# Storing the dv and dk windows of a decode block's backward pass per kv-head

## The chip, the core and the metric

The kernel runs on one core of a Trainium2 chip. TensorE (PE) multiplies, VectorE (DVE) and ScalarE (ACT) work on tiles and empty PSUM, GpSimd (POOL) does some copies and starts transfers, SyncE (SP) only starts transfers. All transfers, whoever starts them, run on the core's 16 DMA engines. The time is device microseconds (us) of one execution; lower is better.

## The reference

One step of a transformer block is computed with its gradients, all in bfloat16, for a batch of B = 4 and one query position:

```python
xn = layernorm(x)                                  # x: [4, 1, 512]
q  = xn @ wq                                       # 32 heads of 128
k, v = last 1024 of the 4096 cached rows           # caches: [4, 8 kv-heads, 4096, 128]
o  = softmax(q k^T / sqrt(128)) v                  # 4 query heads share one kv-head
out = x + o @ wo + (gelu(xn @ w_gate) * (xn @ w_up)) @ w_down
```

The outputs are `out` and the gradients for x, k_cache, v_cache, wq, wo, w_gate, w_up and w_down. The gradients for the two caches (dk and dv) have the caches' full shape: 32 MiB each, of which 24 MiB belong to rows outside the window and are zero, and 8 MiB to the window of 1,024 rows per kv-head.

## The kernel before, in words

**Order of the work.** A feed-forward part (lines 249 to 373) comes first, then an attention part that runs over the four batch entries b (lines 380 to 638), then an end part (lines 640 to 735) that computes `out`, dx, dwo and dwq. A scheduler orders the instructions of PE, ACT, DVE and POOL from the order in the code and from priorities; only SP's queue is kept in the written order (line 78).

**Attention, per b.** `scores(0, b)` and `scores(1, b)` (line 471) transpose K and V with DVE and multiply; `softmax` (line 509) and `softmax_d` (line 536) make P and dS; `odq` (line 567) makes the output and dq; and `dvdk(0, b)` and `dvdk(1, b)` (line 550) make the window parts of dv and dk, 2 MiB for each call.

**dvdk.** For every pair of rows j, four PSUM banks (`kv_ps`, one for each c) receive 16 small matmuls, and `evac` (line 82) copies each bank to a staging tile with ACT or DVE, whichever its running count says is less loaded. A call uses two staging tiles (`stg`, 128 partitions of 8 KiB, four buffers in all, line 74): bank c holds kv-heads 2c and 2c+1, so the first tile has kv-heads 0 to 3 and the second 4 to 7, and every kv-head's part is complete only when the last j has been copied. In a tile, partition m holds, for each of its four kv-heads, eight window rows: 8 x 128 values, 2,048 bytes. Then `result` (line 112) stores the tile: it issues a transfer from POOL with `single_packet=True`. All other large results (dwd, dwu, dwg, dwo, dwq) go out through `result` and the same four staging buffers too.

**Loads.** `load_kv` (line 216) loads one b of K or V as two transfers of 1 MiB, four kv-heads each. The first K comes from SP's queue, all later loads from POOL's. Buffers: V has one (`va`), K two (`ka`, `kb`), so a load waits until `odq` has read the buffer for the last time. `refill` (line 462) is POOL work: eight small copies that lay out one b's query or output-gradient rows before `scores` uses them.

**Zeros.** The 48 MiB of zeros are written by 32 transfers of 1.5 MiB from SP's queue (`zeros`, line 236). They are spread over the kernel: each waits for the one two (later three) before it, and most also wait for a load's landing, or for a softmax or an `odq` to be done (lines 270, 381, 382, 621, 627, 629, 635, 637).

**Queues.** In the profile, q1 is SP's queue, q0 POOL's, q10 ACT's. A transfer from SBUF or to SBUF with 128 partitions is spread over the 16 DMA engines, eight partitions on each.

Of the kernel before, what the change touches and what calls it, by code (L numbers as in the profile page):

```python
# [18 lines left out]
def kernel(  # L19
# [27 lines left out]
    _, G, Sk, Dh = A_k_cache.shape  # L47
# [4 lines left out]
    K0 = Sk - W  # L52
# [7 lines left out]
    J = W // P  # L60
# [21 lines left out]
    def evac(out, in_, n):  # L82

        ca, cd = (190 + n) / 1.2, (130 + n) / 0.96
        eng = "act" if load["act"] + ca <= load["dve"] + cd else "dve"
        load[eng] += ca if eng == "act" else cd
        if eng == "act":
            return nc.scalar.copy(out=out, in_=in_)  # L88
        return nc.vector.tensor_copy(out=out, in_=in_)  # L89
# [11 lines left out]
    def stg_tile():  # L101
        return stage.tile([P, 4096], BF16, name="stg", tag="stg")

    def store(eng, out, in_, kind, apart, **kw):

        d = eng.dma_start(out=out, in_=in_, **kw)  # L106
        for k in apart:
            tc.declare_no_dep(d.ins, group=k, reason="stores write disjoint parts of the outputs")
        tc.add_to_no_dep_group(kind, d.ins)
        return d  # L110

    def result(out, in_):
        return store(nc.gpsimd, out, in_, "rest", ["zeros", "rest"], single_packet=True)

    def mm(out, lhsT, rhs, first=True, last=True, pos=None):
        kw = {} if pos is None else {"tile_position": pos}
        nc.tensor.matmul(out, lhsT=lhsT, rhs=rhs, start=first, stop=last, **kw)  # L117

    def bank(name, tag="w", shape=(P, 512), dt=FP32):
        pool = {"w": ps_w, "x": ps_x}.get(tag, ps_a)  # L120
        return pool.tile(list(shape), dt, name=name, tag=tag)
# [127 lines left out]
    with tc.tile_pool(name="ffn", bufs=1) as ffn:  # L249
# [76 lines left out]
        for h in range(2):  # L326
            stg = stg_tile()
# [9 lines left out]
        for wi, (wsb, dh, og) in enumerate(((wu_sb, dhu, out_7), (wg_sb, dhg, out_6))):  # L337
# [26 lines left out]
            for h in range(2):  # L364
                stg = stg_tile()
# [9 lines left out]
    with tc.tile_pool(name="mid", bufs=1, reuse_waits="tile") as mid:  # L375
# [4 lines left out]
        with tc.tile_pool(name="att", bufs=1, reuse_waits="tile") as att:  # L380
# [169 lines left out]
            def dvdk(k, b, sp, r_):  # L550

                og = (out_3, out_2)[k]
                stg = [stg_tile() for _ in range(2)]
                sv = [s_[:].rearrange("p (g j d) -> p j g d", g=4, j=J) for s_ in stg]
                for j in range(0, J, 2):
                    ps = [bank("kv_ps", "w", (P, 2, 2, Dh)) for _ in range(NQ)]
                    for u in range(2):
                        for c, q in enumerate(quad):
                            mm(ps[c][:, u].rearrange("p g d -> p (g d)"), sp[q, j + u].rearrange("p a m -> p (a m)"),
                               r_[q, b].rearrange("p g d -> p (g d)"), pos=(Q * c, 0))  # L560
                    for c in range(NQ):
                        evac(sv[c // 2][:, j:j + 2, (c % 2) * 2:(c % 2) * 2 + 2, :], ps[c][:], 512)
                for hf in range(2):
                    result(og[b, hf * 4:(hf + 1) * 4, K0:Sk, :].rearrange("g (m j) d -> m g (j d)", j=J),
                           stg[hf][:].rearrange("p (g e) -> p g e", g=4))

            def odq(k, b, pT):

# [44 lines left out]
            for b in range(B):  # L613
                S = scores(0, b)
                if b + 1 < B:
                    dP = scores(1, b)
                    refill(0, b + 1)
                    refill(1, b + 1)
                P_f, P_b, p_done = softmax(S)
                if b == B - 1:  # L620
                    zeros(3, p_done, 3)
                    turn_wq()
                    dP = scores(1, b)
                pT = turned(P_b, 0)
                o_done = odq(0, b, pT)
                if b + 1 < B:
                    zeros((2, 2, 4)[b], load_kv(b + 1, 1, att, "va", nc.gpsimd, single_packet=True))
                else:
                    zeros(2, o_done, 3)
                dvdk(0, b, spread(P_b, 0), rows[1])  # L630
                dS_b = softmax_d(P_f, dP)
                dST = turned(dS_b, 1)
                o_done = odq(1, b, dST)
                if b + 2 < B:
                    zeros(3, load_kv(b + 2, 0, (kap, att)[b % 2], ("ka", "kb")[b % 2], nc.gpsimd, single_packet=True))
                elif b == B - 1:
                    zeros(len(ztodo), o_done, 3)
                dvdk(1, b, spread(dS_b, 1), rows[0])

        with tc.tile_pool(name="end", bufs=1, reuse_waits="tile") as end:  # L640
# [14 lines left out]
            for n in range(KH):  # L655
                t, e, c = n // 8, n // 4 % 2, n % 4
# [59 lines left out]
            for t in range(4):  # L716
                stg = stg_tile()
# [9 lines left out]
            for c in range(C):  # L727
                stg = stg_tile()
# [37 lines left out]
```

## Time and profile before

Time: 285.05 us, median of 3 runs (284.68 to 286.16).

| of the profiled execution | |
|---|---|
| its own time | 284.82 us |
| span from first to last instruction | 283.0 us |
| PE, DVE, ACT, POOL busy | 66%, 58%, 44%, 21% of the span |
| DMA engines, packets' time: SP's queue q1 | 57.0% of 16 engines' span |
| DMA engines, packets' time: POOL's queue q0 | 40.8% of 16 engines' span |
| bytes moved | 112.21 MB (30.93 MB read from HBM, 81.01 MB written) |

How to read it: the page gives the busy share of every engine, then the span in 40 slices of 7.1 us with a digit for each engine (9 is 90% or more), then the DMA queues with their packets, bytes and the time that the packets took, then the chain of waits that ended last, and at last the costliest groups of instructions and the DMA issues with the median time from issue to landing. "out_dram<-stg" is a transfer from a staging tile to HBM, "out_dram<-ztile" one of zeros. A window can be asked for by itself, and then the shares are those of the window.

### The profile page before, as it was taken

Reading aid. Unit: us, or ns where it says so; the run is one execution under the profiler, and the core shown is the slowest. Engines: PE = TensorE matmul, PEld = TensorE weight load, DVE = VectorE, ACT = ScalarE, POOL = GpSimd, SP = SyncE. Lnnn points to the kernel's source line nnn. Section 1 sums busy time; section 2 is a strip of 40 time slices with the busy share of each in tenths; the row PEclk is TensorE's granted clock in tenths of the full one; section 3 lists DMA queues with packets and bytes.
Section 4 is the critical chain, followed back from the end, with each engine's and each line's share of the span. In section 5 each row is a group of like instructions: output and inputs, shape, how many; then the busy total and the mean of one; then the engine's idle time right before and its main releaser. Section 6 shows DMA issues by size and latency. Waiting matters only on the chain.

```text
span 283.0 us, 4400 instructions
## 1 busy us (share of the span) xinstructions
PE 187.6 (66%) x1731; PEld 76.8 (27%) x1733; DVE 165.0 (58%) x309; ACT 124.4 (44%) x245; POOL 60.3 (21%) x135
## 2 busy tenths in 40 slices
PE   0225989859544899759976663923357998944870
PEld 0102344233111543234331341311034232510210
DVE  4779674898798533635257254055496104396970
ACT  2032774740010469744725420802432767454870
POOL 8500000169075313120040060200020020201110
PEclk9999965556955555755555555555555555685555
DMA  6999989999999999999999999999999999999995
GB/s 217 430 446 435 432 317 420 424 430 396 392 428 406 383 357 425 328 365 411 421 419 414 408 427 405 396 422 421 429 382 423 413 410 403 399 415 396 391 397 223
DMA packets 16883, 112.21 MB, mean 396 GB/s; under 512 B 1368, under 2 KB 1632, under 8 KB 11104
## 3 DMA queue, kind: packets, MB, share of 16 engines
q1 hardware_dynamic: 6544, 66.46, 57.0%
q0 software_dynamic: 10176, 45.35, 40.8%
q8 instruction: 13, 0.21, 0.3%
q10 hardware_dynamic: 144, 0.13, 0.2%
q14 instruction: 6, 0.05, 0.0%
HBM read 30.93 MB, written 81.01 MB: 396 GB/s over the span
## 4 chain that ended last, share of the span: by engine, by line
DMA 30%; issue 14%; PE 13%; DVE 9%; ACT 3%; POOL 2%; POOLq 0%; ACTq 0%; DVEq 0%
DMA out_dram<-stg 30%; DVE scr L93 4%; PE kv_ps L117 4%; PE od_ps L117 3%; PE sc_ps L117 2%; PE dwq_ps L117 2%; ACT stg L88 2%; DVE stg L89 1%; POOL out_dram L106 1%; PE ok_ps L117 1%; PE es_ps L117 1%; DVE spr L492 1%; DVE dqs L593 1%; ACT E_f L524 1%; PE nm_ps L117 1%
## 5 line engine op out<-in xcount | busy, mean ns | idle before, releaser
L88 ACT CAST stg<-kv_ps 128x512 bf16<-128x512 f32 x118 | 63.6, 606 | 52.2 <-DMA out_dram<-stg 26.3
L106 POOL DMA_DIRECT2D out_dram<-stg x30 | 19.7, 659 | 150.0 <-ACT stg L88 94.7
L117 PE MATMUL sc_ps<-scr,bd 128*32 128x256 bf16 x256 | 24.2, 396 | 15.2 <-DVE scr L93 15.2
L117 PE MATMUL kv_ps<-qm,spr 32*128 32x256 bf16 x128 | 24.8, 385 | 13.0 <-ACT stg L88 12.5
L117 PE MATMUL kv_ps<-dm,spr 32*128 32x256 bf16 x128 | 28.9, 399 | 6.6 <-ACT stg L88 4.9
L93 DVE STREAM_TRANSPOSE scr<-va 128x1024 uint32<-128x1024 uint32 x16 | 18.9, 1219 | 12.9 <-DMA va<-in_A_v_cache_dram 12.8
L117 PEld LDWEIGHTS <-spr 32*128 32x128 bf16 x256 | 12.4, 102 | 46.4 <-issue 42.1
L89 DVE CAST stg<-kv_ps 128x512 bf16<-128x512 f32 x10 | 6.6, 683 | 17.0 <-PE kv_ps L117 11.0
L117 PEld LDWEIGHTS <-bd 128*32 128x32 bf16 x256 | 8.1, 107 | 29.1 <-issue 28.5
L88 ACT CAST stg<-dwg_ps 128x448 bf16<-128x448 f32 x26 | 12.7, 554 | 6.4 <-PE dwg_ps L117 5.5
L88 ACT CAST stg<-dwo_ps 128x512 bf16<-128x512 f32 x18 | 10.0, 588 | 11.4 <-PE dwo_ps L117 10.1
L117 PE MATMUL dwo_ps<-dy_b,oSP 32*128 32x512 bf16 x32 | 9.0, 508 | 7.5 <-ACT stg L88 6.2
L93 DVE STREAM_TRANSPOSE scr<-ka 128x1024 uint32<-128x1024 uint32 x8 | 9.6, 1228 | 5.2 <-DMA ka<-in_A_k_cache_dram 3.1
L222 POOL DMA_DIRECT2D va<-in_A_v_cache_dram x8 | 6.0, 757 | 27.3 <-PE od_ps L117 25.8
L93 DVE STREAM_TRANSPOSE scr<-kb 128x1024 uint32<-128x1024 uint32 x8 | 9.8, 1232 | 3.5 <-DMA kb<-in_A_k_cache_dram 2.9
L117 PE MATMUL do_ps<-scr,dyBD 128*128 128x512 bf16 x31 | 10.1, 459 | 2.4 <-DVE scr L93 2.1
L578 DVE SCALAR_TENSOR_TENSOR odt<-od_ps,oms,odt 128x128 f32<-128x128 f32 x4 | 1.4, 340 | 17.0 <-ACT odt L577 17.0
L117 PE MATMUL dwq_ps<-dqSP,xn_b 32*128 32x512 bf16 x32 | 10.7, 586 | 0.9 <-ACT stg L88 0.3
L89 DVE CAST stg<-dwq_ps 128x512 bf16<-128x512 f32 x15 | 9.9, 689 | 1.6 <-PE dwq_ps L117 1.4
L89 DVE CAST stg<-dwo_ps 128x512 bf16<-128x512 f32 x14 | 9.2, 680 | 2.7 <-PE dwo_ps L117 2.7
L117 PEld LDWEIGHTS <-pT 128*32 128x32 bf16 x256 | 9.2, 140 | 5.2 <-ACT pT L88 2.3
L88 ACT CAST stg<-dwq_ps 128x512 bf16<-128x512 f32 x17 | 9.7, 586 | 1.4 <-PE dwq_ps L117 0.7
(196 smaller groups left out, 321.3 us busy)
## 6 DMA issues: line engine op xcount, KB each, us to landing
out_dram<-ztile SPq DMA_DIRECT2D x32, 1536.0 KB, 12.1
out_dram<-stg POOLq DMA_DIRECT2D x24, 1024.0 KB, 13.7
va<-in_A_v_cache_dram POOLq DMA_DIRECT2D x8, 1024.0 KB, 17.6
out_dram<-stg POOLq DMA_DIRECT2D x6, 896.0 KB, 10.2
wq_sb<-in_A_wq_dram SPq DMA_DIRECT2D x1, 4096.0 KB, 25.6
wo_sb<-in_A_wo_dram SPq DMA_DIRECT2D x1, 4096.0 KB, 36.7
kb<-in_A_k_cache_dram POOLq DMA_DIRECT2D x4, 1024.0 KB, 19.4
ka<-in_A_k_cache_dram SPq DMA_DIRECT2D x2, 1024.0 KB, 44.3
```

The costliest lines, as they stand in the source:

```text
L88: return nc.scalar.copy(out=out, in_=in_)
L89: return nc.vector.tensor_copy(out=out, in_=in_)
L93: nc.vector.transpose(out=out, in_=in_)
L106: d = eng.dma_start(out=out, in_=in_, **kw)
L117: nc.tensor.matmul(out, lhsT=lhsT, rhs=rhs, start=first, stop=last, **kw)
L222: d = eng.dma_start(out=tl[:, hs].rearrange("p g j d -> p g (j d)"), in_=src[b, hs, K0:Sk, :].rearrange("g (m j) d -> m g (j d)", j=J), **kw)
L492: TS(out=sp[:, :, a, :], in0=src[:].rearrange("p (j m) -> p j m", j=J), scalar1=amask[:, a:a + 1], scalar2=None, op0=ALU.mult)
L524: nc.scalar.activation(out=E_f[:], in_=S, func=ACT.Exp, bias=negm[:, 0:1], scale=1.0, accum_out=es[:])
L578: done = STT(out=t_[:], in0=ps[:, 1, :], scalar=mk[:, 1:2], in1=t_[:], op0=ALU.mult, op1=ALU.add)
L593: nc.vector.tensor_copy(out=dqs[q, :, :, :, a * B + b], in_=d3v[q])
```

## The change

At the end of `dvdk` the two stores of a call, one for each staging tile, become eight stores, one for each kv-head. Each takes 2,048 bytes from each of the 128 partitions of a staging tile and writes 256 KiB that lie together in HBM (the window of one kv-head). Before, a store took 8 KiB from each partition, as four pieces of 2,048 bytes that go to four places in HBM. The bytes, the staging tiles and the copies into them stay as they are.

```diff
-                for hf in range(2):
-                    result(og[b, hf * 4:(hf + 1) * 4, K0:Sk, :].rearrange("g (m j) d -> m g (j d)", j=J),
-                           stg[hf][:].rearrange("p (g e) -> p g e", g=4))
+                for g in range(G):
+                    result(og[b, g, K0:Sk, :].rearrange("(m j) d -> m (j d)", j=J),
+                           stg[g // 4][:, g % 4 * J * Dh:(g % 4 + 1) * J * Dh])
```

## The prediction, made before the result was known

> **What bounds the kernel now.** I read the queues first, then the slices, then the chain of waits. From the page:
>
> ```profile
> DMA  6999989999999999999999999999999999999995
> ...
> DMA packets 16883, 112.21 MB, mean 396 GB/s; under 512 B 1368, under 2 KB 1632, under 8 KB 11104
> ...
> q1 hardware_dynamic: 6544, 66.46, 57.0%
> q0 software_dynamic: 10176, 45.35, 40.8%
> ```
>
> The two large queues fill 97.8% of the time of all 16 DMA engines, and from the second slice to the last but one no digit is under 8. The kernel is bound by its transfers. The chain says the same from the other side:
>
> ```profile
> DMA 30%; issue 14%; PE 13%; DVE 9%; ACT 3%; POOL 2%; POOLq 0%; ACTq 0%; DVEq 0%
> DMA out_dram<-stg 30%; DVE scr L93 4%; PE kv_ps L117 4%; PE od_ps L117 3%; PE sc_ps L117 2%; PE dwq_ps L117 2%; ACT stg L88 2%; DVE stg L89 1%; POOL out_dram L106 1%; PE ok_ps L117 1%; PE es_ps L117 1%; DVE spr L492 1%; DVE dqs L593 1%; ACT E_f L524 1%; PE nm_ps L117 1%
> ```
>
> 30% of the chain waits for stores out of the staging tiles, yet a chain through a store is a wait for bandwidth here: while ACT waits for a tile, SP's zeros use the same engines. So what counts is (a) the DMA time of all bytes and (b) the time in which the engines have nothing. For (b) I asked windows where a slice looked thin (columns: window, length, busy time of PE, PEld, DVE, ACT, POOL, then clock, DMA share, GB/s):
>
> ```profile
> 85.00:95.00 10.00, 4.90 (x89) 2.75 (x88) 7.54 (x14) 1.84 (x5) 4.32 (x20) 0.50 0.93 391
> 115.00:125.00 10.00, 6.51 (x95) 3.31 (x92) 4.68 (x13) 5.15 (x12) 0.76 (x1) 0.55 0.95 324
> 205.00:210.00 5.00, 3.27 (x68) 2.12 (x68) 5.00 (x8) 2.49 (x7) 1.50 (x2) 0.50 0.91 367
> 265.00:280.00 15.00, 9.14 (x29) 2.02 (x26) 9.27 (x15) 8.64 (x15) 2.19 (x5) 0.50 0.94 385
> ```
>
> Idle DMA time: 0.07 x 10 + 0.05 x 10 + 0.09 x 5 + 0.06 x 15 = 2.55 us. Beside it stand only the start and the last 3 us. Nothing that speeds up the stores' owners can win much more than 2.55 us.
>
> **The change part by part.** *Packets.* q0's 10,176 packets can be counted from the code: 44 transfers x 16 engines = 704 completion records; 14 stores with 128 rows of 7 or 8 KiB (dwd, dwu, dwg, dwo, dwq) = 1,792; the other 30 transfers of 1 MiB have 7,680 left, 256 each, so 4,096 bytes a packet: two rows of 2,048 bytes travel as one. On q1 the first K load has the same rows, and there each is a packet of its own (1,024 of 2,048 bytes). The trace's packet records, by size: 4,096 bytes take 160 ns at the median (mean 169, least 156), 2,048 bytes 84 (mean 85, least 84), 12,288 bytes 460, a completion 9. How a store with one row per partition is packed on q0, no row shows. Two neighbours' rows (a packet of 4,096 bytes): 0. One row a packet: 8,192 x 84 - 4,096 x 160 ns on 16 engines = +2.0 us; by the means +0.4, by the least +3.1. Larger packets, now that the HBM side lies together: at the 12,288-byte row's 37 ns per KiB, 4,096 x 10 ns / 16 = -2.6 us. I take 0: every q0 transfer of such rows is packed in pairs, and the flag and the queue stay. The ends -2.6 and +3.1 go into the range.
>
> *Completions.* 16 stores become 64: 48 x 16 records more, 9 ns each, on 16 engines: +0.43 us. Nothing hides this while the engines are full.
>
> *Gaps between transfers.* Two loads that follow each other with no zeros beside them land 2.7 us apart (75 to 80 us, 1 MiB each), and 16 packets at the 160 to 173 ns of that stretch take 2.6 to 2.8: no gap, so 48 more seams cost 0. If each seam cost 0.1 us in the third of the time that q0 is alone, it would be 1.6 us.
>
> The Trainium skill speaks against the change here: "DMA: Bandwidth & Descriptors", sections "Anatomy of one DMA" and "Rules for kernel authors", gives about 2.0 us fixed plus the bytes at 436 GB/s for each transfer and advises 1 MiB or more. Paid in series its fixed part would be an estimated 48 x 2.0 = 96 us. By it the two loads would land 4.4 us apart, and the trace has 2.7; the fixed part lies beside other transfers, and I leave it out.
>
> *POOL.* The issue of a 1 MiB store takes 0.75 us, that of one with 128 rows 0.53 (the end part's):
>
> ```profile
> 243.11 0.76 POOL L106 DMA_DIRECT2D out_dram<-stg  x1 [1.72 <-ACT okT L651]
> 253.72 0.55 POOL L106 DMA_DIRECT2D out_dram<-stg  x1 [9.85 <-DVE pr L704]
> 260.95 0.53 POOL L106 DMA_DIRECT2D out_dram<-stg  x1 [3.85 <-ACT stg L88]
> ```
>
> The new stores have 128 rows: a call issues for 8 x 0.53 = 4.2 us where it took 1.5, +2.7, in eight calls +22 us. POOL is busy 60.3 of 283 us, and 256 KiB per 0.53 us is 495 GB/s, above the 396 that the engines move, so q0 isn't starved. What is queued behind: later loads, and one `refill` (1.8 us at 165.7) that PE needs only at 194, after V has landed. Cost 0; without the cover 2.7 us at one call.
>
> *The ring of semaphores.* In the trace each POOL transfer raises one of eight semaphores in turn, and is issued only when the transfer eight places before has landed; before, POOL never stands for that. Eight stores now fill the ring, so POOL will wait, with a dvdk's last two stores for the load ahead of them. As q0 is first in, first out, the order of the bytes stays. Seven transfers behind the awaited one are at least 1.75 MiB, 4.6 us at 2.6 us per MiB. Cost 0.
>
> *Staging.* If a copy waits only for the quarters that it overwrites, ACT (28.2 us of waits for stores, 7 times) starts earlier; the engines are full then, so 0.
>
> Sum: +0.43 us on the profiled 284.82 = 285.25. The median of the runs is 0.23 above the profiled execution: **285.5 us**.
>
> **The rivals.** *Faster by earlier stores (D).* The first quarter can leave when two copies fewer are done, and tiles come free in quarters. Its most is all idle DMA time: 285.05 + 0.43 - 2.55 = 282.9. For it: the 28.2 us of waits. Against: in 127 to 202 us the engines are full, so a faster ACT only moves zeros.
>
> *Slower by single packets (B).* Place: the 16 MiB of stores. Price: +0.43 + 2.0 = 287.5. Then there is sharing. In 165 to 170 us both queues have work and take turns, one packet each:
>
> ```profile
> q1 hardware_dynamic: 144, 1.57, 73.9%
> q0 software_dynamic: 143, 0.54, 26.6%
> ```
>
> 160 ns against 460 gives q0 26%; 84 against 460 gives it 15%. Zeros would run ahead, and later stretches have nothing beside the attention's own chain: up to the 2.55 us of idle again, 290. It decides as soon as q0's packets stand near 10,176 + 768 + 4,096 = 15,040, not 10,944.
>
> The same page, section "SWDGE vs HWDGE vs iDMA", says that packets on GpSimd's path have preferably at most 4,096 bytes and up to 64 descriptors. The 4,096-byte packets fit that, the 8 KiB rows exceed it; by it pairs across partitions are allowed, and this case's cost would be 0.
>
> *Slower by the ring (C).* POOL stands for a landing, q0 runs dry behind it, and each of some six hand-overs (a load and its stores) loses an issue, 0.53 us, plus one refill of 1.8: 5.0 us. q1 fills the engines for 57% of the time: 2.2 left, 287.7 with the completions, 290.5 without zeros beside. It decides where the landing on the slowest engine comes over 4.6 us after the others have drained their seven. Against: zeros stand by.
>
> That the change does nothing but add completions (A) is the forecast.
>
> **How the numbers follow.** A 0.52, B 0.24, C 0.13, D 0.11. The bound for a difference that a measurement can tell is 0.5%, 1.4 us: 283.6 to 286.5. A lies inside it for 0.45, above it for 0.05 (seams, POOL), below for 0.02 (larger packets). B is inside with 0.03 (the means' +0.4) and above with 0.21. C 0.02 and 0.11. D 0.03 and, below, 0.08. Together: faster 0.10, same 0.53, slower 0.37. Range: low 283.6 leaves out the larger part of D and the large packets; high 289.0 takes in B and C up to the part with lost sharing; about 0.18 is left out.
>
> **What would show it.** Right: q0 10,944 packets and its share within 0.5% of 40.8; idle DMA time near 2.5 us; 64 + 14 store issues near 0.53 us; GpSimd waiting for its own transfers, with no thin slice to match. B: 15,040 packets, and about 26% falling to 15% where both queues have work. C: DMA shares below 0.9 behind such waits. D: thin windows gone. Wrong altogether, if the scheduler orders ACT and PE anew and opens an idle stretch that no term here has, or if HBM takes 256 KiB in one place at another rate than pieces 1 MiB apart: then the 4,096-byte packets' 160 ns would move.

## The result and the profile after

The changed kernel takes **289.18 us** (median of 6 runs, 287.02 to 293.11) where the kernel before took 284.90 in the same comparison: ratio **1.013 [1.009, 1.0169]**, slower. (The ratio leaves out the run of 293.11 us, which lies over 1.5% above the fastest of this kernel.) The forecast was 285.5, within 283.6 to 289.0. The profiled execution took 288.74 us, span 286.7 against 283.0. From its page (the last line is the group of all stores: count, busy time, mean ns; then POOL's idle time ahead of them):

```profile
DMA  6999989999999999999999999999999999999995
...
DMA packets 17652, 112.22 MB, mean 391 GB/s; under 512 B 2136, under 2 KB 2400, under 8 KB 11872
...
q1 hardware_dynamic: 6544, 66.46, 56.6%
q0 software_dynamic: 10944, 45.36, 40.8%
...
DMA 37%; PE 13%; DVE 9%; ACT 6%; issue 5%; POOL 2%; POOLq 0%; ACTq 0%; DVEq 0%
DMA va<-in_A_v_cache_dram 19%; DMA out_dram<-stg 17%; DVE scr L93 5%; ACT stg L88 4%; PE kv_ps L117 3%; PE dwq_ps L117 2%; PE dwo_ps L117 2%; PE od_ps L117 2%; DVE dqs L593 2%; POOL out_dram L106 2%; PE sc_ps L117 1%; PE dqr_ps L117 1%; POOL va L222 1%; PE es_ps L117 1%; ACT E_f L524 1%
...
L106 POOL DMA_DIRECT2D out_dram<-stg x78 | 42.1, 544 | 139.8 <-ACT stg L88 74.5
```

q0 has 10,944 packets, to the packet what the forecast named, and the slices look as full as before. So no single packets and no thin slices show. (A full slice does not say that POOL's queue had work: zeros can fill the engines. The experiments come back to this.) The chain's share of DMA has risen from 30% to 37%, and loads of V, which the chain of before did not name, now lead it with 19%, ahead of the stores' 17%. Windows, the four of the forecast and the thinnest new one:

```profile
85.00:95.00 10.00, 6.17 (x106) 3.64 (x105) 6.98 (x17) 2.35 (x7) 2.66 (x11) 0.50 0.97 406
115.00:125.00 10.00, 6.79 (x96) 3.32 (x96) 3.46 (x12) 5.21 (x13) 1.76 (x3) 0.50 0.95 320
180.00:185.00 5.00, 0.68 (x13) 0.20 (x2) 1.74 (x3) 0.82 (x2) 1.71 (x4) 0.50 0.89 352
205.00:210.00 5.00, 4.17 (x50) 1.23 (x49) 2.84 (x5) 4.55 (x10) 0.78 (x2) 0.50 0.98 378
265.00:280.00 15.00, 13.05 (x40) 2.88 (x39) 12.66 (x20) 12.40 (x23) 2.66 (x5) 0.50 0.94 386
```

The four hold 0.30 + 0.50 + 0.10 + 0.90 = 1.80 us of idle DMA time (2.55 before), the new one 0.55. All packets' times, divided by 16, sum to 280.86 us against 278.38: 0.42 us of the rise are completion records, the rest packets that took 1 to 2% longer (4,096 bytes 172.1 ns for 169.4, 12,288 bytes 476.9 for 472.4). Idle is the rest of the span, 5.8 for 4.7 us. This account adds up to the 3.7 us of span, but it does not say what waited for what. Three other views do.

**POOL's queue.** POOL's waits (times in us: total, count, longest) now name landings, which before did not hold a single store:

```profile
POOL out_dram L106 <- DMA out_dram<-stg: 21.6, 12, 3.5
...
POOL out_dram L106 <- DMA va<-in_A_v_cache_dram: 10.1, 3, 6.9
```

The scheduler also put POOL's calls in another order. In units of 256 KiB: before va, 4 stored, ka, 8, va, 4, kb, 8, va, 8, `refill`, 32; after va, 5, ka, 5, va, 4, kb, 4, va, 14, `refill`, 32. By the last load of V 24 quarters had been stored before, 18 after. POOL's timeline, before:

```profile
125.54 1.50 POOL L222 DMA_DIRECT2D va<-in_A_v_cache_dram  x2 [7.35 <-PE od_ps L117]
127.03 0.76 POOL L106 DMA_DIRECT2D out_dram<-stg  x1
143.45 1.49 POOL L222 DMA_DIRECT2D kb<-in_A_k_cache_dram  x2 [15.66 <-PE od_ps L117]
```

and after:

```profile
143.88 1.51 POOL L222 DMA_DIRECT2D kb<-in_A_k_cache_dram  x2 [13.55 <-PE od_ps L117]
145.39 0.56 POOL L106 DMA_DIRECT2D out_dram<-stg  x1
146.90 0.56 POOL L106 DMA_DIRECT2D out_dram<-stg  x1 [0.95 <-DMA va<-in_A_v_cache_dram]
```

The second tile of `dvdk(1, 0)` was stored at 127.03 before and landed at 150.7. After, its last two quarters stand behind kb's load, which waits 13.55 us for `odq` to be done with the buffer: issued at 145.39 and 146.90, landed at 164.2 and 167.0.

**The copies into staging.** The last `dvdk` call's copies on ACT, before:

```profile
231.18 2.05 ACT L88 CAST stg<-kv_ps 128x512 bf16<-128x512 f32 x4 [0.24 <-ACT pT L88]
233.69 1.07 ACT L88 CAST stg<-kv_ps 128x512 bf16<-128x512 f32 x2
```

and after:

```profile
231.07 1.07 ACT L88 CAST stg<-kv_ps 128x512 bf16<-128x512 f32 x2 [0.24 <-ACT pT L88]
238.04 1.07 ACT L88 CAST stg<-kv_ps 128x512 bf16<-128x512 f32 x2 [5.90 <-DMA out_dram<-stg]
```

Both start at 231. After, ACT then stands 5.90 us for a landing, and the attention's last copy ends at 247.9 us in place of 242.1. The tile it waits for was stored by `dvdk(1, 2)`, whose eight quarters went out at 209.8 to 213.7 and landed at 218.0 to 237.9, one every 2.8 us. Before, its two stores went out at 206.2 and 207.5 and landed at 216.2 and 225.6. The few us in issue became twelve in landing, since zeros ran beside them (before, q0 had over 60% of the engines from 207 to 213 us). The DMA queues of the changed kernel from 220 to 225 us:

```profile
q1 hardware_dynamic: 141, 1.54, 74.6%
q0 software_dynamic: 139, 0.45, 23.7%
```

Packet for packet in turns, 139 to 141, but zeros' packets are three times as large: the stores get a quarter of the engines. Of the 139, 30 are completion records, so they take turns too, and a divided store has more of them. (The Trainium skill, "DMA: Bandwidth & Descriptors", section "Queues, rings and completion order", says that an engine takes turns between queues at packet granularity; these counts agree.)

**The end part.** It begins with dwo, whose PSUM blocks are copied to the same staging buffers. What held dwo's copies (us, times), in the changed kernel:

```profile
L88 ACT CAST stg<-dwo_ps x18: 585/585/605, 251.1 to 267.5; 128x512 bf16<-128x512 f32 x18
...
  PE dwo_ps L117: 11.8, 14
  ACT stg L88: 5.2, 9
  DVE nm L702: 0.9, 1
```

No transfer is among them. From the attention's last copy to the end of the span it is 38.8 us, in this kernel a chain of PE, ACT and DVE. Before it was 41.0, with one wait of 1.3 us for a store. So the kernel ends at the later of two times: the transfers', and that of the attention plus about 39 us. Before, by this estimate, the second lay some 2 us (41.0 - 38.8) ahead of the first.

### The profile page after: what moved, and what is told of

Its sections match the earlier page's. It is cut to its first block, busy times and chain, and to the rows that moved or that the text cites. A ratio compares the mean times of both kernels' runs of the same rounds, so it can differ in the third digit from the quotient of the medians.

```text
span 286.7 us, 4497 instructions
## 1 busy us (share of the span) xinstructions
PE 187.9 (66%) x1733; PEld 75.6 (26%) x1733; DVE 165.7 (58%) x309; ACT 124.0 (43%) x245; POOL 83.0 (29%) x183
## 3 DMA queue, kind: packets, MB, share of 16 engines
q0 software_dynamic: 10944, 45.36, 40.8%
## 4 chain that ended last, share of the span: by engine, by line
DMA 37%; PE 13%; DVE 9%; ACT 6%; issue 5%; POOL 2%; POOLq 0%; ACTq 0%; DVEq 0%
DMA va<-in_A_v_cache_dram 19%; DMA out_dram<-stg 17%; DVE scr L93 5%; ACT stg L88 4%; PE kv_ps L117 3%; PE dwq_ps L117 2%; PE dwo_ps L117 2%; PE od_ps L117 2%; DVE dqs L593 2%; POOL out_dram L106 2%; PE sc_ps L117 1%; PE dqr_ps L117 1%; POOL va L222 1%; PE es_ps L117 1%; ACT E_f L524 1%
## 5 line engine op out<-in xcount | busy, mean ns | idle before, releaser
L106 POOL DMA_DIRECT2D out_dram<-stg x78 | 42.1, 544 | 139.8 <-ACT stg L88 74.5
L117 PE MATMUL kv_ps<-qm,spr 32*128 32x256 bf16 x128 | 26.8, 396 | 18.6 <-ACT stg L88 17.0
```

## The experiments

**Theories.** *Ring*: the eight semaphores let POOL have eight transfers under way; divided stores make that a quarter of the bytes, POOL stands, staging comes free later. *Order*: the scheduler's new order of POOL's queue does it. Rivals: *transfer* (256 KiB pieces are dearer in themselves, the kernel is bound by its transfers) and *POOL time* (the +22 us of issue). All ratios are against the kernel before, run beside each kernel. All "last copy" and "tail" figures (end of the attention's last copy; from there to the end of the span) come from the profiled executions.

| kernel | median us | ratio [95%] | span | last copy | tail |
|---|---|---|---|---|---|
| before | 284.90 | 1 | 283.0 | 242.1 | 41.0 |
| changed | 289.18 | 1.013 [1.009, 1.0169] | 286.7 | 247.9 | 38.8 |
| e1 two stores, order of before by hand | 283.68 | 0.9965 [0.993, 1.0] | 281.1 | 232.6 | 48.5 |
| e2 eight stores, same order | 287.98 | 1.0102 [1.0064, 1.0141] | 287.7 | 248.4 | 39.3 |
| e3 two stores, order of after by hand | 288.14 | 1.0107 [1.0072, 1.0142] | 284.0 | 245.5 | 38.6 |
| e4 four stores | 287.07 | 1.0052 [1.0025, 1.0078] | 286.1 | 247.3 | 38.8 |
| e5 two stores, ring filled | 289.24 | 1.0133 [1.0088, 1.0178] | 287.3 | 246.1 | 41.2 |
| e6 two stores, POOL busy | 285.27 | 0.9969 [0.9935, 1.0003] | 280.6 | 234.9 | 45.8 |
| e7 e1, fewer zeros | 279.08 | 0.9747 [0.9695, 0.9798] | 277.5 | 235.0 | 42.5 |
| e8 changed, fewer zeros | 287.39 | 1.0067 [1.0029, 1.0104] | 284.6 | 245.9 | 38.7 |
| e9 two stores, ahead of loads | 285.82 | 1.0001 [0.9963, 1.0038] | 283.8 | 228.5 | 55.3 |
| e10 eight stores, ahead of loads | 286.32 | 1.0037 [1.0003, 1.0071] | 284.6 | 230.7 | 53.8 |

**e1 and e2: the order fixed, the stores undivided or divided.** POOL's queue is written by hand in the order of before; finished stores wait in a list until their place comes (`PRE` and `POST`: kv-heads' parts to store before and after the two `dvdk` calls of each b). Some memsets, the refills and the last store of dwg were moved to fit.

```diff
-    ctx.enter_context(tc.manual_schedule(engines={nc.sync.engine}))
+    ctx.enter_context(tc.manual_schedule(engines={nc.sync.engine, nc.gpsimd.engine}))
...
-                    result(og[b, hf * 4:(hf + 1) * 4, K0:Sk, :].rearrange("g (m j) d -> m g (j d)", j=J),
-                           stg[hf][:].rearrange("p (g e) -> p g e", g=4))
+                    pend.append((og[b, hf * 4:(hf + 1) * 4, K0:Sk, :].rearrange("g (m j) d -> m g (j d)", j=J),
+                                 stg[hf][:].rearrange("p (g e) -> p g e", g=4)))
...
+            PRE, POST = [(0, 0), (0, 8), (8, 0), (0, 0)], [(4, 8), (4, 0), (8, 8), (8, 8)]
...
+                flush(PRE[b][0])
                 dvdk(0, b, spread(P_b, 0), rows[1])
+                flush(POST[b][0])
```

e2 has this with the eight stores of the change; the orders of ACT, DVE and SP are the same in both, that of PE differs in a few places.

> Two stores for each dvdk call, as before the change, but POOL's queue written out by hand in the order that the scheduler gave it before (in MiB of window stores between the loads: va, 1, ka, 2, va, 1, kb, 2, va, 2, the last refill, 8). All theories: 0.99 to 1.01 of before, span 281 to 286 us. It is the base for the other fixed orders. If it is off by more than 1%, the fixed order changes something else, and the others are read against this one alone.

> Eight stores for each call, in the same fixed order of POOL's queue as the run with two. Ring theory (POOL issues a transfer only when the transfer eight places before has landed, so stores are held behind a load's landing, the staging tiles come free late and the end part starts late): 2 to 5 us above the fixed run with two stores, POOL waits for DMA landings of 20 us or more, the last copy out of kv_ps 2 to 6 us later. Order theory (the scheduler put loads ahead of finished stores in POOL's queue, and that alone makes them late): within 1 us of the fixed run with two. Transfer theory (48 more completions and more time for each packet): 0.4 to 2.6 us above, with no later end of the attention than that.

e1 is at 0.9965, e2 at 1.0102: 1.0137 apart (1.0102 / 0.9965), 4.3 us in the medians, with the order of POOL's queue unchanged. The order is not the sole cause. In e1 no store waits for a landing; in e2:

```profile
POOL out_dram L106 <- DMA out_dram<-stg: 27.8, 12, 4.6
POOL out_dram L106 <- DMA va<-in_A_v_cache_dram: 18.2, 3, 10.4
```

and ACT's longest wait for a staging tile, 9.96 us, stands where the changed kernel has its 5.90, ahead of the last call's copies at 238.5.

**e3: undivided stores in the order of after.** As near as 1 MiB stores allow:

```diff
-            PRE, POST = [(0, 0), (0, 8), (8, 0), (0, 0)], [(4, 8), (4, 0), (8, 8), (8, 8)]
+            PRE, POST = [(0, 0), (4, 4), (16, 0), (0, 0)], [(4, 4), (0, 0), (8, 8), (8, 8)]
```

> Two stores for each call, with POOL's queue in the order that the scheduler gave the changed kernel, as nearly as stores of 1 MiB can follow it (va, 1, ka, 1, va, 1, kb, 1, va, 4, refill, 8 MiB). Order theory: 3 to 5 us above the fixed run with two stores in the old order. Ring theory: within 1 us of it, as a ring of eight holds 8 MiB of such stores. Transfer theory: the same as the fixed run with two.

1.0107: the order costs as much as the division alone (e2), with no store waiting for a landing. (Its profiled execution took 286.09 us, the lowest of its six runs, so its span stands low beside its median.) `dvdk(1, 1)` ends its copies at 173.1 us here, at 176.2 in the changed kernel, at 156.7 before and 155.9 in e1. This is not POOL's order by itself: with it the scheduler also put twelve of the sixteen copies of `dvdk(1, 1)` behind the next b's softmax, here as in the changed kernel (softmax starts on ACT at 154.75 and 155.82 us); before and in e1 all sixteen stand ahead of it. Late stores and this new order were not tested apart. The two causes, order and division, do not add: each pushes the attention's last copy to 245 to 248 us.

**e4: four stores of 512 KiB**, scheduler's order.

```diff
-                for hf in range(2):
-                    result(og[b, hf * 4:(hf + 1) * 4, K0:Sk, :].rearrange("g (m j) d -> m g (j d)", j=J),
-                           stg[hf][:].rearrange("p (g e) -> p g e", g=4))
+                for g in range(0, G, 2):
+                    result(og[b, g:g + 2, K0:Sk, :].rearrange("g (m j) d -> m g (j d)", j=J),
+                           stg[g // 4][:, g % 4 * J * Dh:(g % 4 + 2) * J * Dh].rearrange("p (g e) -> p g e", g=2))
```

> Four stores of 512 KiB for each call (two kv-heads each), order left to the scheduler, which puts the loads as far ahead of the stores as in the changed kernel (va, 1.5, ka, 1, va, 1, kb, 1, va, 3.5, refill, 8 MiB). Order theory: as slow as the changed kernel, ratio 1.010 to 1.016. Ring theory: between, 1.002 to 1.009, as the ring holds twice the bytes. Transfer theory: a third of the change's loss, 1.003 to 1.006.

1.0052, between the two and within what the ring theory named, but the transfer theory's 1.003 to 1.006 holds it as well; only the order theory misses.

**e5: the ring filled without divided stores.** To e1 three transfers of a few bytes are added behind each 1 MiB store:

```diff
+                    for _ in range(3):
+                        n_ = len(small_done)
+                        small_done.append(nc.gpsimd.dma_start(out=idle[:, n_, :], in_=A_x.rearrange("b s (p e) -> (b s p) e", p=4)[:, 0:4], single_packet=True))
```

**e6: POOL busy without transfers.** To e1 eight memsets are added for each store:

```diff
+                    for _ in range(8):
+                        nc.gpsimd.memset(idle[:], 0.0)
```

> As the kernel with two stores and POOL's queue written by hand in the order of before (283.68 us), but each 1 MiB store is followed by three POOL transfers of 8 bytes for each of 4 partitions or so (a few bytes of x into a tile that nobody reads; added work). Eight places of the ring of semaphores go by in a call, as with eight stores, while the large transfers stay at 1 MiB. Ring theory: POOL waits for landings of out_dram<-stg for 10 to 35 us, and the time is 286 to 289, as with eight stores in that order (287.98). Transfer theory (256 KiB pieces themselves are dearer): POOL's waits do not count, 283 to 285.

> The kernel with two stores in the order of before (283.68 us), with eight memsets of a 128 x 128 tile on POOL ahead of or behind each store (added work): POOL's busy time rises by about what the eight stores' issues added, 15 to 25 us, without a place of the ring more. If the dearer issue is what the eight stores cost: 286 to 288. Ring theory: POOL's time is hidden, 283 to 285.

e5 is at 1.0133, the same as the changed kernel, with every large store undivided. e6 is at 0.9969, though POOL is busy for 87.4 us in place of e1's 59.9. The scheduler orders PE, ACT and DVE in e5 and e6 nearly alike, and a little unlike e1, so e6 is e5's control: 1.0133 / 0.9969 = 1.0164. POOL's waits in e5 (L581 is the added transfer):

```profile
POOL out_dram L106 <- DMA out_dram<-stg: 13.4, 3, 9.6
POOL idle L581 <- DMA va<-in_A_v_cache_dram: 11.9, 3, 8.4
POOL idle L581 <- DMA kb<-in_A_k_cache_dram: 10.2, 2, 7.6
POOL idle L581 <- DMA ka<-in_A_k_cache_dram: 9.1, 2, 6.2
```

A transfer of a few bytes stands for the landing of a load eight places ahead, and the 1 MiB stores stand behind it. So neither the size of the pieces nor POOL's time is needed: the number of POOL's transfers makes a loss of the same size.

The packets show two ways from there to late stores. The first is the ring: a store whose copies ended at 180.2 us is issued only at 188.60, behind V's landing and a `refill`, and the queue runs dry before its packets come. From 190.5 to 193 us q0 moves 7 packets and q1 97; the engines stay full, with zeros. In e2 it is 26 to 92 from 193 to 195.5 us. The second is turns: behind the store that lands at 225.67 us in e5 the three added transfers land at 226.60, 227.53 and 228.51, 0.9 us each with zeros beside, and the next store comes behind them. e5 fills places of the ring and adds turns at once, so how the loss divides between the two is open.

Packets were dearer too: over the engines they sum to 280.1 us in e5 for 276.6 in e6, and to 281.6 in e2 for 276.9 in e1, each in one execution (e2's is among its slower ones, e6's among its faster). That this sets the changed kernel's end is what e8 speaks against.

**e7 and e8: the last two transfers of zeros left out**, from e1 and from the changed kernel.

```diff
-                    zeros(len(ztodo), o_done, 3)
+                    zeros(len(ztodo) - 2, o_done, 3)
```

> The kernel with two stores in the order of before (283.68 us) without the last two transfers of zeros (3 MiB less, those rows are not written). In its profile the attention's last copy ended at 232.6 and the end 48.5 us behind it, so the transfers set its end. Theory of two bounds (the end is the later of the transfers' end and of the attention's last copy + 39 us): 7.9 us less at 2.6 us for each MiB, down to 275 to 278. A plain sum over the engines gives the same here.

> The changed kernel (289.18 us) without the last two transfers of zeros (3 MiB less, those rows are not written). Theory of two bounds: its attention ends at 247.9 and the end part takes 38.8 us behind it, so the bytes taken out from the last stretch bring little, 0 to 3 us: 286 to 289. If the changed kernel is bound by its transfers all the same (dearer packets, idle engines): 7.9 us less, 280 to 282.5.

Against before, e1 falls from 0.9965 to 0.9747, the changed kernel from 1.013 to 1.0067. At 285.05 us that is 6.2 us and 1.8 us, for the same 3 MiB. e7 lost less than 7.9 us and ended 1 us above its expectation: with its bytes gone it meets the other bound, and its tail is 42.5 us. From 250 to 260 us, e7:

```profile
250.00:260.00 10.00, 6.33 (x22) 1.27 (x22) 6.16 (x10) 6.05 (x12) 1.09 (x2) 0.50 0.71 292
```

and e8:

```profile
250.00:260.00 10.00, 5.61 (x27) 1.55 (x25) 9.28 (x20) 5.26 (x11) 0.54 (x1) 0.77 0.51 196
```

In e8 the engines stand half idle (DMA share 0.51) while DVE works 9.28 of 10 us: the changed kernel's end is not set by its transfers. Against the changed kernel's profile the span is 2.1 us shorter because the attention's last copy comes 2.0 us earlier; the tail stays. In e1 the transfers do set the end; there dwo's copies wait for stores:

```profile
L88 ACT CAST stg<-dwo_ps x18: 585/585/605, 235.9 to 261.4; 128x512 bf16<-128x512 f32 x18
...
  DMA out_dram<-stg: 18.2, 5
```

**e9 and e10: every call's stores ahead of the next load**, two or eight.

```diff
-            PRE, POST = [(0, 0), (0, 8), (8, 0), (0, 0)], [(4, 8), (4, 0), (8, 8), (8, 8)]
+            PRE, POST = [(0, 0), (0, 0), (0, 0), (0, 0)], [(8, 8), (8, 8), (8, 8), (8, 8)]
```

> Two stores, POOL's queue written by hand as in the kernel of 283.68 us, but every call's stores stand ahead of the next load instead of behind it. Theory: what counts is when the staging tiles come free, so stores that never wait behind a load free them at least as early, and a load of V or K that starts later costs only if the scores wait for it: 282 to 285, with the attention's last copy at 230 to 238. Rival (loads are what the attention waits for; they now stand behind ACT's copies): 286 to 289, with DVE's or PE's waits for va, ka or kb in the front.

> The same order with eight stores. Ring theory in its plain form (eight transfers under way at most, 256 KiB each, are too small a queue): 286 to 289, 2 to 5 us over the kernel with two stores in this order, with POOL waits for out_dram<-stg of 10 us and more. Rival (the ring only hurts where a store waits for a load ahead of it): with the stores ahead of the loads within 1.5 us of the kernel with two stores in this order.

e9 is at 1.0001, within its expected 282 to 285 only by its lower runs (median 285.82, 283.3 to 287.35); its attention ends first of all, at 228.5 us, and that brings nothing, as transfers then set the end, 55.3 us later. e10 is 1.0036 above it (1.0037 / 1.0001; 0.5 us in the medians, and the two intervals overlap), so the ring theory in its plain form falls. POOL in e10 stands for landings as long as anywhere:

```profile
POOL out_dram L106 <- DMA va<-in_A_v_cache_dram: 26.2, 5, 8.9
POOL out_dram L106 <- DMA out_dram<-stg: 19.3, 11, 2.9
POOL out_dram L106 <- DMA kb<-in_A_k_cache_dram: 9.3, 2, 6.5
POOL out_dram L106 <- DMA ka<-in_A_k_cache_dram: 7.4, 2, 4.9
```

62.2 us, against 61.1 in e2 (with 8.3 for ka and 6.8 for kb). But the `dvdk` copies wait for staging tiles for only 3.7 us here and not at all in e9, against 24.1 in e2, and the attention ends at 230.7. (dwo's copies, behind the attention, wait 28.6 us here and 28.3 in e9.) So a standing POOL costs nothing by itself, and neither do the turns of 48 more transfers. They cost where a copy needs the tile whose store stands behind, and where the attention's end sets the end.

e1 is the fastest of the kernels here that write every row (e7 and e8 leave 3 MiB of zeros out). That it beats the changed kernel is clear; against the kernel before its interval touches 1.0, and e6, the same order with more work on POOL, has 0.9969 [0.9935, 1.0003]. More staging buffers for the changed kernel, the direct cure, were not tried.

## Why the prediction was right or wrong, point by point

The forecast was +0.43 us, and the ratio of 1.013 on 285.05 us is +3.7: 288.8, inside the range by 0.2 (the plain median, 289.18, lies just above it). That is luck: the range reached up to 289.0 for the sake of B and C, not of the sum, and "same" had the largest chance where 1.3% is clear of the 0.5% that it called the bound. Nearly all of its signs of being right came, 10,944 packets, q0's share of 40.8%, issues of 0.54 us, POOL waiting for its own transfers with no thin slice to match, and the time was another all the same: none of them looks at when the attention ends.

- **The bound** ("The kernel is bound by its transfers") was half of it. e7 shows it true of two undivided stores with little to spare; e8 shows the changed kernel on the other side. The forecast took the 97.8% as leave to price every later store at nothing. The step that failed is its sentence "a chain through a store is a wait for bandwidth here": the attention's end starts a chain of 39 us that no transfer shortens, and before it had about 2 us to spare.
- **The ring** ("Cost 0") is the term that was mis-sized. It was described correctly: eight semaphores, and a dvdk's last two stores waiting for the load ahead of them. But "as q0 is first in, first out, the order of the bytes stays" looked at bytes and not at who waits for them. Its cover of 4.6 us was about right and too short: in e2 V's load lands at 188.08 us and the seven stores behind it are through at 192.44, but after one store more a `refill` comes first, the next stores are issued from 190.69 on, and q0 is nearly dry from 193 to 195.5. Measured for more transfers as a whole, ring and turns: 1.0137 (e2 over e1), and 1.0164 (e5 over e6).
- **Rival C** (287.7 to 290.5, chance 0.13) comes nearest and holds the time. Its q0 running dry is seen in e2 and e5; in the changed kernel no stretch behind a wait of POOL's is as clear. Its sign, shares under 0.9, fails, as zeros fill the engines: one window only, 180 to 185 us, has 0.89. Its price is another too, idle engines where the loss is zeros taking the engines while stores come late, and staging after that. Its "Against: zeros stand by" was in fact the harm.
- **POOL's order.** "Later loads" were named as queued behind the stores, but not that the scheduler would put loads ahead of stores. The clause on what would make it wrong named a new order of ACT and PE; that came as well, beside POOL's. e3: 1.0107 for the order, ACT's included.
- **Staging** ("If a copy waits only for the quarters"): the condition did not hold. A copy waits for the whole tile: the first copy of `dvdk(1, 1)` into its first tile is at 147.90, after the last of that tile's four quarters landed at 147.84. ACT's waits for stores rose from 28.2 to 36.9 us, and the 0 put on them was wrong.
- **Packets** (0): right to the packet. (The low end of -2.6 us was a slip: 460 ns over 12 KiB are 38.3 ns per KiB, which makes -1.7; the range's low end did not rest on it.) Rival B falls; q0 has 10,944, not 15,040.
- **Completions** (+0.43): the records of that kind sum to 1.18 us in place of 0.76, +0.42. Right as time of the engines; the turns that they take from the stores were in no term. In e10 over e9, where staging is not late, the whole cost of dividing is about that: 0.5 us in the medians, 0.7 in the spans. The fixed 2.0 us for each transfer that the Trainium skill gives ("DMA: Bandwidth & Descriptors", section "Anatomy of one DMA"), 96 us in series by the estimate, is not seen in it; the advice of 1 MiB or more in its section "Rules for kernel authors" pointed the right way, but what these runs show behind it is the queue.
- **Gaps** (0): no sign of any. Eight quarters with no zeros beside land 0.6 to 0.7 us apart.
- **POOL's issue** (0.53 us a store, +22 us, cost 0): 0.544 and +22.7 us (83.0 for 60.3), and e6 adds 27.5 us of POOL work at no cost. Right.
- **Rival D** did not come: ACT's waits grew, and the 0.75 us of idle that went from the four windows came back elsewhere.

## What to carry to other kernels

Count a queue in bytes as well as in places: where the framework lets eight transfers be under way, dividing a transfer by four divides by four what the queue holds, and the transfers behind it leave later. Beside another queue every transfer, however small, also takes turns. Full DMA engines do not make a late store free. Ask which copy needs its tile, what the kernel still has to do after that copy, and how far this second path lies behind the transfers; here it was 2 us. A scheduler may also answer a change of shapes with another order, so fix the order by hand before a change of size is judged, and see whether the other engines' orders stay.

## What the runs showed of the hardware

- **A late store loses much more than its delay.** With zeros beside, 256 KiB land every 2.8 us (218.0 to 237.9 us in the changed kernel), without them every 0.6 to 0.7 (238.4 to 243.2). Here the same store beside zeros takes four times as long.
- **Zeros' packets differ by up to 4% in their mean, and why is open.** The 12,288-byte packets have a mean of 471.1 ns in e1 and 485.5 in e2, 473.7 in e9 and 479.5 in e10, but also 467.5 in e6 and 477.9 in e5, where no store is divided, and 472.3 in e8, where every store is, as in the kernel before (472.4). The median is 460 or 461 in every run, so some slow packets make the difference. These are single executions; a rule does not come out of them. In e10 packets' times raise the sum over the engines by 2.8 us over e9 (281.06 for 278.22, 0.42 of it completions), of which the span shows 0.7, as idle time shrank from 5.6 to 3.5 us.
